# Retention ahead of two MoE layers on one core: output products of one kind for all five chunks together, tail scores one product per head

## The chip, the cores and the metric

The kernel runs on one core of a Trainium2 chip. The time is the device time of one execution in microseconds (us); of several executions the median is given. TensorE multiplies matrices: a *weight load* brings the stationary operand into the array, the matmul then streams the moving operand through it. In the profile TensorE is PE (its weight loads PEld, which overlap the matmuls), VectorE is DVE, ScalarE is ACT, GpSimd is POOL. PSUM is the memory that TensorE writes its results to, SBUF the one that it reads from. Each engine carries out its own instructions in order; between engines, semaphores order the work.

## The reference

```python
def _attn_ref(q, k, v):                  # q, k, v: 4 batches x 8 heads x 576 tokens x 64
    B, H, S, D_ = q.shape
    scores = (1.0 / np.sqrt(D_)) * np.matmul(q, k.transpose(0, 1, 3, 2))
    gamma = 1.0 - 2.0 ** (-5.0 - np.arange(H, dtype=np.float32))
    rel = np.arange(S)[:, None] - np.arange(S)[None, :]
    Dmat = np.where(rel >= 0, gamma[:, None, None] ** rel[None, :, :], 0.0)
    return np.matmul(scores * Dmat[None, :, :, :], v).astype(np.float32)

def _moe_ref(x, w_in, w_out):            # x: 2304 x 512, d_ff 2048
    h = x @ w_in
    g = np.maximum(0.01 * h, h)
    return (g @ w_out).astype(np.float32)

def _moe2_ref(x, w_in, w_out):
    h = x @ w_in
    g = h - np.tanh(h)
    return (g @ w_out).astype(np.float32)

def reference(...):
    attn_out = _attn_ref(q, k, v)
    x = attn_out.transpose(0, 2, 1, 3).reshape(B * S, H * D)
    x = _moe_ref(x, moe w_in, moe w_out)
    return _moe2_ref(x, moe2 w_in, moe2 w_out)
```

## The kernel before

The retention works on 16 *pairs* (batch, two heads): two heads of 64 values fill the 128 partitions. The 576 tokens are NFULL = 4 chunks of 128 and a tail of 64 (so NCH = 5 chunks). Within a chunk the scores are masked products of k and q; what lies before a chunk reaches it through a state `st`, a 64 x 64 matrix per head and chunk. The states' summands come from TensorE into `c_` (a view of the PSUM tile `x_c`), and `states` (L670) adds them up: ACT copies the first (L673), DVE makes the three sums after it (L675). The output of a chunk is *far* (state times q, `outputs_far`, L697) plus *near* (masked scores `pt` times v, `outputs_near`, L708), both added in PSUM: chunks 0 to 3 in the tile `o`, the tail in `x_t`. `finish` (L713) splits the output into a rounded high part `xh` (ACT, L716) and the rest `xl` (DVE, L717), the first layer's inputs.

One step of the loop over the pairs, for pair i, in program order: its four chunks' scores (`scores`, L632, 8 products with 64 rows of weights), q scaled in place by a table on POOL (`prep_q`, L602 for the chunks, L607 for the tail), the mask (L646, DVE), a part of `fill`, then `pair_steps` (L805): outputs of pair i - 1, the states' products of pair i (`states_mm`, L665), the tail's scores (`scores_tail`, L638), the states, `finish` of pair i - 1 for the tail (`x_t`) and then for the chunks, the mask of the tail (L655, DVE), and for pair i + 1 `prep_tail` (L621, ACT) and the scaling of k (`prep_k`, L613, ACT).

The tail's scores of both heads are one product of 128 rows: the weights are k of both heads, the moving operand is `bd`, a block-diagonal copy of the tail's q (two tiles `bds`, zeros outside the blocks, the two blocks copied by `prep_tail`). `x_e` is a PSUM tile of three parts of 64 columns: two for the tail's scores `x_a`, one for the tail's output `x_t`; `c_` lies in a PSUM tile of its own.

From pair 5 on (`fast`), `pair_steps` first runs a *unit* of the first MoE layer on 256 tokens: `unit_h(u)` (L758, 24 products of 128 rows into `x_b`, then L764 to L766 on ACT and DVE) and `unit_o(u - 1)` (L783, 24 products into `a`, then L802 and L803). `fill` emits pieces of the preparation of weights between these steps, by the table `marks`: ACT L166, DVE L172, L177 and L183 (rounding in integer arithmetic), ACT L255 (the high part of a weight) and POOL L256 (the low part). A unit's products read both parts.

The order of each engine is the order in which the program is written. The tile framework adds a semaphore wait wherever an instruction uses a tile that another engine used before. From 150.4 us on the layers follow, over all tokens (L275, L309, L428); the change does not touch them.

Of the kernel before, what the change touches and what calls it, by code (L numbers as in the profile page):

```python
# [10 lines left out]
F32 = mybir.dt.float32  # L11
# [3 lines left out]
AF = mybir.ActivationFunctionType  # L15
# [3 lines left out]
P = 128  # L19
CH = 128  # L20
# [15 lines left out]
def retention_moe_moe(  # L36
# [16 lines left out]
    nc = tc.nc  # L53
    B, NP, _, S = qT.shape
# [3 lines left out]
    NFULL = S // CH  # L58
    TAIL = S - NFULL * CH
    NCH = NFULL + 1  # L60
    MAIN = NFULL * CH
# [493 lines left out]
    def retention():  # L555
        with ExitStack() as ac:
            ak = ac.enter_context(tc.tile_pool(name="ak", bufs=1))
            ap_ = ac.enter_context(tc.tile_pool(name="ap", bufs=3))
            cw_pool[0] = ac.enter_context(tc.tile_pool(name="c0", bufs=2))
            ps_s = ac.enter_context(tc.tile_pool(name="ps_s", bufs=1, space=PSUM))  # L560
            ps_a = ac.enter_context(tc.tile_pool(name="ps_a0", bufs=1, space=PSUM))

            x_e = ps_s.tile([P, 3, TAIL], F32, name="x_e")
            x_a, x_t = x_e[:, :2, :], x_e[:, 2, :]
            x_b = ps_s.tile([P, 2, QW], F32, name="x_b")
            x_c = ps_s.tile([P, 512], F32, name="x_c")
            c_ = x_c[:, :NFULL * 64].rearrange("p (c d) -> p c d", d=64)


            cm_sb = ak.tile([P, NP, 2, CH], F32, name="cm_sb")  # L570
# [2 lines left out]
            sts = [ak.tile([P, NFULL, 64], F32, name=f"st{i}") for i in range(2)]  # L573
            decay = ak.tile([P, NP], F32, name="decay")
            pt_ = [ak.tile([P, 2, S], F32, name=f"pt{i}") for i in range(2)]
            bds = [ak.tile([P, 2, TAIL], F32, name=f"bd{i}") for i in range(2)]
            qk, kv, pts = {}, {}, {}
            order = [(b, p) for b in range(B) for p in range(NP)]

# [18 lines left out]
            def prep_q(i):  # L598

                b, p = order[i]  # L600
                q = qk[i][:, 1, :MAIN].rearrange("p (c r) -> p c r", r=CH)
                nc.gpsimd.tensor_tensor(  # L602
                    out=q, in0=q, in1=qt_sb[:, p:p + 1, :].to_broadcast([P, NFULL, CH]),
                    op=ALU.mult,
                )
                q = qk[i][:, 1, MAIN:]
                nc.gpsimd.tensor_tensor(out=q, in0=q, in1=qt_sb[:, p, :TAIL], op=ALU.mult)  # L607

            def prep_k(i):
                b, p = order[i]  # L610
                for h in range(2):
                    k = kv[i][:, :NFULL, 64 * h:64 * h + 64]
                    nc.scalar.activation(out=k, in_=k, func=AF.Copy, scale=kt_sb[:, p, h:h + 1])  # L613

            def prep_tail(i):

                q = qk[i][:, 1, MAIN:]
                for h in range(2):
                    o = slice(64 * h, 64 * h + 64)
                    if i:  # L620
                        nc.scalar.activation(out=bds[i % 2][o, h, :], in_=q[o], func=AF.Copy)  # L621
                    else:
                        nc.vector.tensor_copy(out=bds[i % 2][o, h, :], in_=q[o])

            def scores(i):
                kt, qt = qk[i][:, 0, :], qk[i][:, 1, :]
# [8 lines left out]
                return sc  # L635

            def scores_tail(i):
                nc.tensor.matmul(  # L638
                    out=x_a, lhsT=qk[i][:, 0, S - CH:], rhs=bds[i % 2], start=True, stop=True
                )  # L640

            def mask(i, sc):
                b, p = order[i]
# [26 lines left out]
            def states(i):  # L670
                b, p = order[i]
                st = sts[i % 2]
                nc.scalar.activation(out=st[:, 0, :], in_=c_[:, 0, :], func=AF.Copy)  # L673
                for c in range(1, NFULL):
                    nc.vector.scalar_tensor_tensor(  # L675
                        out=st[:, c, :], in0=st[:, c - 1, :], scalar=decay[:, p:p + 1],
                        in1=c_[:, c, :], op0=ALU.mult, op1=ALU.add,
                    )

            def chunk_out(o_, c):  # L680
                n = min(CH, S - c * CH)
                cs = slice(c * CH, c * CH + n)
                return (o_[:, cs] if c < NFULL else x_t), cs
# [6 lines left out]
            def outputs_far(i, o_, chunks):  # L690

                q, st = qk[i][:, 1, :], sts[i % 2]
                for c in chunks:
                    dst, cs = chunk_out(o_, c)
                    for h in range(2):
                        o = slice(64 * h, 64 * h + 64)
                        nc.tensor.matmul(  # L697
                            out=dst[o], lhsT=st[o, c - 1, :], rhs=q[o, cs],
                            start=c in (1, NFULL), stop=False, skip_group_check=True,
                        )  # L700

            def outputs_near(i, o_, chunks):
                pt, t = pts[i], kv[i]
                for c in chunks:
                    dst, cs = chunk_out(o_, c)
                    for h in range(2):
                        o = slice(64 * h, 64 * h + 64)
                        nc.tensor.matmul(  # L708
                            out=dst[o], lhsT=t[:, NFULL + c, o], rhs=pt[:, h, cs],
                            start=False, stop=True, skip_group_check=True,  # L710
                        )
# [21 lines left out]
            def fill(i, part):  # L733
                a, b = marks[i:i + 2] if i < len(order) else marks[-1:] * 2
                now = a + (b - a) * (part + 1) // 3
                for op in ops[done[0]:now]:
                    op()
                done[0] = max(done[0], now)
# [12 lines left out]
            def unit_h(u):  # L751
                t0, f0 = place(u)
                for f in range(2):
                    w = wt[0, 0, f0 + f]
                    for kk in range(KK):
                        cs = slice(kk * P, (kk + 1) * P)
                        for j, (wi, x) in enumerate(((0, xh), (0, xl), (1, xh))):
                            nc.tensor.matmul(  # L758
                                out=x_b[:, f, :], lhsT=w[:, wi, cs], rhs=x[:, kk, t0:t0 + QW],
                                start=f == 0 and kk == 0 and j == 0,  # L760
                                stop=f == 1 and kk == KK - 1 and j == 2, skip_group_check=True,
                            )
                gt = slot(N_OUT + u % 2, True).rearrange("p i (f n) -> p i f n", f=2)
                nc.scalar.activation(out=gt[:, 0], in_=x_b, func=AF.Prelu, alpha=0.01)  # L764
                nc.scalar.activation(out=x_b, in_=x_b, func=AF.Prelu, alpha=0.01)
                nc.vector.tensor_tensor(  # L766
                    out=gt[:, 1], in0=x_b, in1=gt[:, 0].bitcast(F32), op=ALU.subtract
                )
                gs[u] = gt
# [21 lines left out]
            def unit_evac(u):  # L791
                t0, f0 = place(u)
                if f0 == 0 and u >= SPLIT:
                    return
                ps = accs.pop(t0)
                dst = acc_t[:, :, t0:t0 + QW]
                if f0 and u < SPLIT:
                    for d in (0, 2):
                        part = dst[:, d:d + 2]
                        nc.vector.tensor_tensor(out=part, in0=ps[:, d:d + 2], in1=part, op=ALU.add)  # L800
                    return
                nc.scalar.activation(out=dst[:, 2:], in_=ps[:, 2:], func=AF.Copy)  # L802
                nc.vector.tensor_copy(out=dst[:, :2], in_=ps[:, :2])  # L803

            def pair_steps(i, fast):  # L805

                nonlocal u
                if fast:
                    unit_h(u)
                    fill(i, 1)  # L810
                    if u:
                        unit_o(u - 1)
                        unit_evac(u - 1)
                    u += 1
                if i:
                    ot = o_place(i - 1)
                    outputs_far(i - 1, ot, range(1, NFULL))
                    outputs_near(i - 1, ot, range(NFULL))
                    outputs_far(i - 1, ot, [NFULL])
                    outputs_near(i - 1, ot, [NFULL])  # L820
                    del qk[i - 1]
                    del pts[i - 1], kv[i - 1]
                if i < len(order):
                    states_mm(i)
                    scores_tail(i)
                    states(i)
                if i:
                    finish(i - 1, x_t, MAIN, S)
                    finish(i - 1, ot[:, :MAIN], 0, MAIN)
                if i < len(order):  # L830
                    mask_tail(i)
                if i + 1 < len(order):
                    prep_tail(i + 1)
                    prep_k(i + 1)

            t = ap_.tile([P, 2, S], F32, tag="qk", name="qk")
# [11 lines left out]
            nc.vector.memset(qb[:, 0:1], -RHO_V * math.sqrt(RHO_C))  # L848
            nc.vector.memset(qb[:, 1:2], -TANH_T * TANH_T)
            nc.scalar.activation(out=qb[:, 3:4], in_=qb[:, 2:3], func=AF.Tanh)  # L850
            for t in bds:
                nc.vector.memset(t, 0.0)
            for t in pt_:
                nc.vector.memset(t[:LATE, :, MAIN:], 0.0)
            for p in range(NP):
                for h in range(2):
                    nc.vector.memset(
                        decay[64 * h:64 * h + 64, p:p + 1], float(gamma[2 * p + h] ** CH)
                    )
            prep_tail(0)  # L860
            prep_k(0)
            for i in range(len(order)):
                if i + 1 < NP:
# [249 lines left out]
```

## Time and profile before

| | |
|---|---|
| Time before, median of 3 runs | 868.3 us (867.96 to 868.88) |
| Profiled execution, its own time | 868.1 us |
| Span of its trace | 866.1 us |
| Mean granted clock of TensorE | 0.998 |
| Busy: PE, PEld, DVE, ACT, POOL | 850.1, 748.2, 604.1, 451.2, 377.1 us |

The span runs from the first to the last instruction of the trace; the execution's own time is 2.0 us longer. The busy times are sums over the whole span, in which the retention has the first 150 us. What an engine's busy time is worth depends on the stretch: the view of busy times by stretch shows them one by one, the timeline shows single instructions with the engine's idle time ahead of them and what ended it.

### The profile page before, as it was taken

What the parts mean: (1) busy time and instruction counts of PE and PEld (TensorE: products, weight loads), DVE (VectorE), ACT (ScalarE), POOL (GpSimd) and SP (SyncE); (2) the same over time, 40 slices, a digit from 0 to 9 for tenths busy, and PEclk for the clock granted to TensorE, in tenths of its full rate; (3) what the DMA queues carried; (4) which work ended last, traced back from release to release, by engine and by line L of the source; (5) the groups of instructions that cost most, each with busy time, mean ns of one, the idle gap of its engine ahead of it and who ended that gap; (6) DMA issues with size and microseconds to landing.
All of it is one profiled execution on the core that took longest, in us unless ns stands there. A gap on an engine that the chain in (4) does not pass through costs nothing.

```text
span 866.1 us, 15237 instructions
## 1 busy us (share of the span) xinstructions
PE 850.1 (98%) x5728; PEld 748.2 (86%) x5728; DVE 604.1 (70%) x1038; ACT 451.2 (52%) x899; POOL 377.1 (44%) x304
## 2 busy tenths in 40 slices
PE   6999999999999999999999999999999999999997
PEld 5889999888888889888888898888999899999996
DVE  5995767587786676658765577756676667777675
ACT  4553444453255433454444577666556566566663
POOL 2541222040036302464365379655545445545553
PEclk9999999999999999999999999999999999999999
DMA  9835663433454533644444503572225412563112
GB/s 340 315 125 172 219 209 118 150 121 103 135 213 186 179 121 110 243 170 127 190 175 165 195 1 146 226 284 75 75 96 180 162 73 74 208 231 121 49 50 74
DMA packets 38778, 134.43 MB, mean 155 GB/s; under 512 B 4400, under 2 KB 5936, under 8 KB 36656
## 3 DMA queue, kind: packets, MB, share of 16 engines
q1 hardware_dynamic: 38272, 133.25, 43.7%
q8 instruction: 45, 0.74, 0.4%
q14 instruction: 29, 0.24, 0.1%
q10 hardware_dynamic: 432, 0.20, 0.1%
HBM read 97.26 MB, written 36.18 MB: 154 GB/s over the span
## 4 chain that ended last, share of the span: by engine, by line
PE 89%; DVE 4%; DMA 2%; issue 2%; POOL 1%; ACT 1%; POOLq 0%; ACTq 0%; SPq 0%; DVEq 0%
PE a L428 40%; PE h L275 22%; PE h L309 17%; PE a L783 3%; PE x_b L758 3%; PE o L708 1%; PE sc L632 1%; PE o L697 1%; DVE cw L183 1%; DMA acc<-in_w1i 1%; DMA cm_sb<-in_cmask 1%; DVE pt L646 1%; PE x_c L665 0%; DVE v L394 0%; DMA kt_sb<-in_ktab 0%
## 5 line engine op out<-in xcount | busy, mean ns | idle before, releaser
L428 PE MATMUL a<-w 128*128 128x512 f32 (+1 forms) x1680 | 395.2, 377 | 0.5 <-POOL w L400 0.5
L428 PEld LDWEIGHTS a<-w 128*128 128x128 f32 x1680 | 293.1, 188 | 48.9 <-POOL w L400 1.3
L256 POOL TENSOR_TENSOR w<-cw,w 128x512 fp32r<-128x512 f32 x80 | 113.5, 1436 | 233.6 <-ACT w L255 207.8
L275 PE MATMUL h<-xh,w 128*128 128x512 f32 (+1 forms) x672 | 187.1, 349 | 0.0
L368 POOL TENSOR_TENSOR v<-t,u 128x512 f32<-128x512 f32 (+1 forms) x76 | 93.1, 1225 | 100.5 <-ACT t L365 96.4
L275 PEld LDWEIGHTS h<-xh,w 128*128 128x128 f32 x672 | 119.5, 188 | 17.0
L400 POOL TENSOR_TENSOR w<-v,w 128x512 fp32r<-128x512 f32 (+1 forms) x76 | 96.1, 1265 | 63.9 <-ACT w L399 63.9
L354 ACT ACTIVATE w<-h 128x512 fp32r<-128x512 f32 (+1 forms) x68 | 37.2, 547 | 160.3 <-PE h L275 115.4
L275 PE MATMUL h<-xl,w 128*128 128x512 f32 (+1 forms) x336 | 117.0, 348 | 0.0
L309 PE MATMUL h<-xh,w 128*128 128x256 f32 x512 | 100.9, 281 | 0.2
L309 PEld LDWEIGHTS h<-xe,w 128*128 128x128 f32 x576 | 80.8, 189 | 10.7 <-DVE mk L303 3.1
L183 DVE SCALAR_TENSOR_TENSOR cw<-st,cw 128x512 uint32<-128x512 uint32 x96 | 86.4, 900 | 2.5
L394 DVE SCALAR_TENSOR_TENSOR v<-q,v 128x512 f32<-128x512 f32 (+1 forms) x76 | 60.8, 800 | 37.1 <-POOL v L368 37.1
L364 ACT ACTIVATE u<-h 128x512 f32<-128x512 f32 (+1 forms) x80 | 44.2, 553 | 80.4 <-DVE h L303 53.2
L309 PEld LDWEIGHTS h<-xh,w 128*128 128x128 f32 x512 | 83.1, 190 | 2.8 <-DVE v L397 1.5
L309 PE MATMUL h<-xe,w 128*128 128x256 f32 x576 | 84.3, 282 | 1.1 <-DVE mk L303 1.0
L505 DVE TENSOR_TENSOR acc<-a,acc 128x512 f32<-128x512 f32 (+1 forms) x114 | 72.1, 657 | 18.5 <-PE a L428 18.5
L399 ACT ACTIVATE w<-v 128x512 fp32r<-128x512 f32 (+1 forms) x76 | 45.3, 596 | 61.5 <-DVE v L397 59.0
L172 DVE TENSOR_SCALAR cw<-cw 128x512 f32<-128x512 f32 x64 | 33.1, 518 | 57.7 <-ACT cw L166 57.6
L309 PE MATMUL h<-xl,w 128*128 128x256 f32 x256 | 71.8, 281 | 0.0
L275 PEld LDWEIGHTS h<-xl,w 128*128 128x128 f32 x336 | 63.3, 188 | 8.6
L383 DVE TENSOR_TENSOR h<-h,t 128x512 f32<-128x512 f32 (+1 forms) x80 | 51.3, 641 | 15.2 <-ACT t L365 15.2
(82 smaller groups left out, 1159.8 us busy)
## 6 DMA issues: line engine op xcount, KB each, us to landing
kept<-w SPq DMA_DIRECT2D x48, 512.0 KB, 3.5
w<-kept SPq DMA_DIRECT2D x48, 512.0 KB, 4.8
xe<-xkept SPq DMA_DIRECT2D x12, 1536.0 KB, 6.7
st<-in_w2i SPq DMA_DIRECT2D x16, 512.0 KB, 3.5
st<-in_w1i SPq DMA_DIRECT2D x12, 512.0 KB, 4.1
st<-in_w1o SPq DMA_DIRECT2D x12, 512.0 KB, 3.5
xkept<-xe SPq DMA_DIRECT2D x4, 1536.0 KB, 6.7
kv<-in_vn SPq DMA_DIRECT2D x16, 320.0 KB, 5.2
```

The costliest lines, as they stand in the source:

```text
L183: nc.vector.scalar_tensor_tensor(out=t["w"], in0=t[src], scalar=scalar, in1=t["w"], op0=op, op1=ALU.bitwise_or)
L256: nc.gpsimd.tensor_tensor(out=wp[:, 1, :], in0=wf, in1=wp[:, 0, :].bitcast(F32), op=ALU.subtract)
L275: nc.tensor.matmul(out=ps[:, :n], lhsT=w[:, wi, cs], rhs=x[:, kk, t0:t0 + n], start=kk == 0 and i == 0, stop=kk == KK - 1 and i == 2,)
L309: nc.tensor.matmul(out=out_, lhsT=w[:, wi_, at:at + P], rhs=x(xi, kk), start=start and kk == 0 and j == 0, stop=stop and kk == 1 and j == ...
L364: nc.scalar.activation(out=u[:, :n], in_=h, func=AF.Square)
L368: nc.gpsimd.tensor_tensor(out=v[:, :n], in0=t_[:, :n], in1=u[:, :n], op=ALU.mult)
L383: nc.vector.tensor_tensor(out=h, in0=h, in1=tmp[s][1][:, :n], op=ALU.subtract)
L394: nc.vector.scalar_tensor_tensor(out=v, in0=q, scalar=RHO_A, in1=v, op0=ALU.add, op1=ALU.mult)
L399: nc.scalar.activation(out=gt[:, 0, g_at(s)], in_=v, func=AF.Copy)
L400: (nc.gpsimd if m else nc.vector).tensor_tensor(out=gt[:, 1, g_at(s)], in0=v, in1=gt[:, 0, g_at(s)].bitcast(F32), op=ALU.subtract)
L428: nc.tensor.matmul(out=o, lhsT=l, rhs=r, start=f == 0 and i == 0 and d % pack == 0, stop=f == GF - 1 and i == 2 and (d + 1) % pack == 0, s ...
L505: nc.vector.tensor_tensor(out=dst, in0=a, in1=dst, op=ALU.add)
```

## The change

The three-part tile `x_e` becomes a tile of two PSUM banks of 512 columns. `x_a` takes the first 64 columns of either bank (a head in each), `x_t` the next 64 of the first bank, and `c_` 256 columns of the second. The tiles `x_c` and `bds` go. The tail's scores are now one product per head, with 64 rows of weights and the tail's q itself as the moving operand (after L631), so the copies by `prep_tail` go. `prep_tail` is now the name of POOL's scaling of the tail's q (after L608), which has to come after the tail's scores and is written behind them. The outputs come as far for chunks 1 to 4, then near for chunks 0 to 4 (after L691, L702).

```diff
-            x_e = ps_s.tile([P, 3, TAIL], F32, name="x_e")
-            x_a, x_t = x_e[:, :2, :], x_e[:, 2, :]
+            x_e = ps_s.tile([P, 2, 512], F32, name="x_e")
+            x_a, x_t = x_e[:, :, :TAIL], x_e[:, 0, TAIL:2 * TAIL]
             x_b = ps_s.tile([P, 2, QW], F32, name="x_b")
-            x_c = ps_s.tile([P, 512], F32, name="x_c")
-            c_ = x_c[:, :NFULL * 64].rearrange("p (c d) -> p c d", d=64)
+            c_ = x_e[:, 1, TAIL:TAIL + NFULL * 64].rearrange("p (c d) -> p c d", d=64)
...
-            bds = [ak.tile([P, 2, TAIL], F32, name=f"bd{i}") for i in range(2)]
...
+
+            def prep_tail(i):
+                b, p = order[i]
                 q = qk[i][:, 1, MAIN:]
                 nc.gpsimd.tensor_tensor(out=q, in0=q, in1=qt_sb[:, p, :TAIL], op=ALU.mult)
...
-            def prep_tail(i):
-
-                q = qk[i][:, 1, MAIN:]
-                for h in range(2):
-                    o = slice(64 * h, 64 * h + 64)
-                    if i:
-                        nc.scalar.activation(out=bds[i % 2][o, h, :], in_=q[o], func=AF.Copy)
-                    else:
-                        nc.vector.tensor_copy(out=bds[i % 2][o, h, :], in_=q[o])
...
             def scores_tail(i):
-                nc.tensor.matmul(
-                    out=x_a, lhsT=qk[i][:, 0, S - CH:], rhs=bds[i % 2], start=True, stop=True
-                )
+                for h in range(2):
+                    r = slice(64 * h, 64 * h + 64)
+                    nc.tensor.matmul(
+                        out=x_a[:, h, :], lhsT=qk[i][r, 0, S - CH:], rhs=qk[i][r, 1, MAIN:],
+                        start=True, stop=True,
+                    )
...
-                    outputs_far(i - 1, ot, range(1, NFULL))
-                    outputs_near(i - 1, ot, range(NFULL))
-                    outputs_far(i - 1, ot, [NFULL])
-                    outputs_near(i - 1, ot, [NFULL])
+                    outputs_far(i - 1, ot, range(1, NCH))
+                    outputs_near(i - 1, ot, range(NCH))
                     del qk[i - 1]
                     del pts[i - 1], kv[i - 1]
                 if i < len(order):
                     states_mm(i)
                     scores_tail(i)
+                    prep_tail(i)
                     states(i)
...
-                    prep_tail(i + 1)
                     prep_k(i + 1)
...
-            for t in bds:
-                nc.vector.memset(t, 0.0)
...
-            prep_tail(0)
             prep_k(0)
```

PE's order in pair 3 before, from the last far product of pair 2 to the scores of pair 4 (a product is written as output, moving operand and weights, then rows x columns; in brackets the semaphores that it waits for, by engine or DMA queue):

```order
L697 MATMUL o<-qk,st_92 64x128
L708 MATMUL o<-pt_95,kv 64x128 x8
L697 MATMUL x_e<-qk,st_92 64x64 [waits DVE_49,Pool_49]
L697 MATMUL x_e<-qk,st_92 64x64
L708 MATMUL x_e<-pt_95,kv 64x64 x2
L665 MATMUL x_c<-kv 64x64 [waits DMAHW7_49,DMAHW0_49,Activation_49]
L665 MATMUL x_c<-kv 64x64 [waits Activation_49]
L665 MATMUL x_c<-kv 64x64 x6
L638 MATMUL x_e<-bd_98,qk 128x128
L632 MATMUL sc<-qk 128x128 [waits DMAHW4_49,DMAHW5_49,DVE_49,PE_49]
```

The same place after:

```order
L691 MATMUL o<-qk,st_91 64x128
L691 MATMUL x_e<-qk,st_91 64x64 [waits DVE_49,Pool_49]
L691 MATMUL x_e<-qk,st_91 64x64
L702 MATMUL o<-pt_94,kv 64x128 x8
L702 MATMUL x_e<-pt_94,kv 64x64 x2
L659 MATMUL x_e<-kv 64x64 [waits DMAHW7_49,DMAHW0_49,Activation_49]
L659 MATMUL x_e<-kv 64x64 [waits Activation_49]
L659 MATMUL x_e<-kv 64x64 x6
L631 MATMUL x_e<-qk 128x64 x2
L623 MATMUL sc<-qk 128x128 [waits DMAHW4_49,DMAHW5_49,DVE_49,PE_49]
```

The far products of the tail moved ahead of the near ones, and the tail's scores became two products that read q itself.

ACT's order in pair 6 before, from the copy of the first state on:

```order
L673 ACTIVATE st_92<-x_c 128x64 [waits PE_49]
L716 ACTIVATE xh<-x_e 128x64 [waits PE_49]
L716 ACTIVATE xh<-o 128x512
L621 ACTIVATE bd_98<-qk 64x64 [waits DMAHW3_49]
L621 ACTIVATE bd_98<-qk 64x64
L613 ACTIVATE kv<-kv,kt_sb 128x4x64 [waits DMAHW5_49]
L613 ACTIVATE kv<-kv,kt_sb 128x4x64
L255 ACTIVATE w<-cw 128x512 [waits DVE_49]
```

The same place after:

```order
L667 ACTIVATE st_91<-x_e 128x64 [waits PE_49]
L710 ACTIVATE xh<-x_e 128x64 [waits DVE_49]
L710 ACTIVATE xh<-o 128x512
L614 ACTIVATE kv<-kv,kt_sb 128x4x64 [waits DMAHW5_49]
L614 ACTIVATE kv<-kv,kt_sb 128x4x64
L255 ACTIVATE w<-cw 128x512
```

The two copies of q are gone, and the first `xh` waits for a count of DVE instead of PE; by the built program's counts that is the third state sum (after L669) of the same pair.

POOL's order before, from q's scaling of pair 5 to that of pair 6:

```order
L602 TENSOR_TENSOR qk<-qk,qt_sb 128x512 [waits DMAHW1_49,DMAHW7_49,PE_49,Pool_49]
L607 TENSOR_TENSOR qk<-qk,qt_sb 128x64 [waits Activation_49]
L256 TENSOR_TENSOR w<-cw,w 128x512 [waits Activation_49] x2
L602 TENSOR_TENSOR qk<-qk,qt_sb 128x512 [waits DMAHW6_49,PE_49,Pool_49]
L607 TENSOR_TENSOR qk<-qk,qt_sb 128x64
```

The same place after:

```order
L600 TENSOR_TENSOR qk<-qk,qt_sb 128x512 [waits DMAHW1_49,DMAHW7_49,PE_49,Pool_49]
L256 TENSOR_TENSOR w<-cw,w 128x512 [waits Activation_49]
L608 TENSOR_TENSOR qk<-qk,qt_sb 128x64 [waits PE_49]
L256 TENSOR_TENSOR w<-cw,w 128x512 [waits DVE_49,Activation_49]
L600 TENSOR_TENSOR qk<-qk,qt_sb 128x512 [waits DMAHW6_49,PE_49,Pool_49]
```

The tail's scaling moved behind the first low part of a weight, and waits for PE's tail scores.

## Rows read from the trace of the kernel before

**Rows 1.** The chain of work that ended last: shares of the span by engine.

```profile
PE 89%; DVE 4%; DMA 2%; issue 2%; POOL 1%; ACT 1%; POOLq 0%; ACTq 0%; SPq 0%; DVEq 0%
```

**Rows 2.** Busy by stretch: us, busy PE PEld DVE ACT POOL, PEclk, DMA, GB/s.

```profile
18.00:58.00 40.00, 36.36 (x463) 31.88 (x460) 38.82 (x74) 23.78 (x57) 21.54 (x19) 1.00 0.68 244
...
66.20:150.40 84.20, 84.20 (x988) 77.13 (x988) 59.64 (x111) 36.59 (x89) 22.69 (x22) 1.00 0.55 179
150.40:866.00 715.60, 709.14 (x4035) 621.25 (x4033) 491.30 (x808) 380.17 (x726) 326.31 (x252) 1.00 0.40 143
```

**Rows 3.** Timeline, weight loads of one pair: start, us, engine, line, operation, idle before.

```profile
86.41 0.63 PEld L697 LDWEIGHTS o<-qk,st 64*64 64x64 f32 x12
87.21 0.85 PEld L708 LDWEIGHTS o<-pt,kv 128*64 128x64 f32 x16 [0.17 <-issue]
88.23 0.20 PEld L697 LDWEIGHTS x_e<-qk,st 64*64 64x64 f32 x4 [0.17 <-issue]
88.50 0.20 PEld L708 LDWEIGHTS x_e<-pt,kv 128*64 128x64 f32 x4
88.61 0.55 PEld L665 LDWEIGHTS x_c<-kv 128*64 128x64 f32 x16
89.23 0.30 PEld L638 LDWEIGHTS x_e<-bd,qk 128*128 128x128 f32 x2
89.65 0.97 PEld L632 LDWEIGHTS sc<-qk 64*128 64x128 f32 x16
90.74 0.19 PEld L758 LDWEIGHTS x_b<-xh,w 128*128 128x128 f32 x1
```

**Rows 4.** The same view, the last pair's tail scores and the unit behind.

```profile
139.16 0.30 PEld L638 LDWEIGHTS x_e<-bd,qk 128*128 128x128 f32 x2
139.38 0.19 PEld L758 LDWEIGHTS x_b<-xh,w 128*128 128x128 f32 x1
```

**Rows 5.** Timeline of DVE, pair 2: state sums, second xl, tail's mask.

```profile
19.99 0.90 DVE L675 SCALAR_TENSOR_TENSOR st<-st,decay,x_c 128x64 f32<-128x64 f32 x3
...
20.94 0.68 DVE L717 TENSOR_TENSOR xl<-o,xh 128x512 fp32r<-128x512 f32 x1
21.63 0.29 DVE L655 TENSOR_TENSOR pt<-x_e,cm_sb 64x128 f32<-64x128 f32 x1
```

**Rows 6.** Timeline of ACT, pair 6.

```profile
47.48 0.22 ACT L716 ACTIVATE xh<-x_e 128x64 fp32r<-128x64 f32 x1 [0.19 <-PE x_e L638]
47.60 0.59 ACT L716 ACTIVATE xh<-o 128x512 fp32r<-128x512 f32 x1
48.08 0.51 ACT L621 ACTIVATE bd<-qk 64x64 f32<-64x64 f32 x2
48.62 0.91 ACT L613 ACTIVATE kv<-kv,kt_sb 128x256 f32<-128x256 f32 x2
49.43 0.61 ACT L255 ACTIVATE w<-cw 128x512 fp32r<-128x512 f32 x1
```

**Rows 7.** Timeline, pair 6: state sums, a weight's low part, and PE behind it.

```profile
49.24 0.90 DVE L675 SCALAR_TENSOR_TENSOR st<-st,decay,x_c 128x64 f32<-128x64 f32 x3
50.12 1.28 POOL L256 TENSOR_TENSOR w<-cw,w 128x512 fp32r<-128x512 f32 x1 [4.41 <-ACT w L255]
51.46 0.30 PEld L758 LDWEIGHTS x_b<-xh,w 128*128 128x128 f32 x2 [1.06 <-POOL w L256]
```

**Rows 8.** Timeline of DVE and POOL, between the sums of pairs 5 and 6.

```profile
41.05 2.63 DVE L183 SCALAR_TENSOR_TENSOR cw<-acc,cw 128x512 uint32<-128x512 uint32 x2
...
46.98 1.40 DVE L183 SCALAR_TENSOR_TENSOR cw<-acc,cw 128x512 uint32<-128x512 uint32 x2
41.37 1.76 POOL L602 TENSOR_TENSOR qk<-qk,qt_sb 128x512 f32<-128x512 f32 x1
43.09 0.77 POOL L607 TENSOR_TENSOR qk<-qk,qt_sb 128x64 f32<-128x64 f32 x1
```

**Rows 9.** Timeline, pair 7: PE's last wait for a low part.

```profile
64.86 1.24 PEld L783 LDWEIGHTS a<-w 128*128 128x128 f32 x10 [0.47 <-POOL w L256]
```

## The prediction

> **What bounds the kernel now.** Three views were read, in this order. First the chain of work that ended last: PE carries 89% of it [rows 1]. That is an average over stages, so next the busy times by stretch [rows 2]. In the layers, from 150.4 us on, PE is busy 709 of 716 us. In the pairs from 66.2 to 150.4 us it is busy all 84.2 us while DVE has 59.6; there a microsecond taken off PE is a microsecond of the kernel. From 18 to 58 us it is DVE that is full, 38.8 of 40 us, and PE has gaps; there only what DVE ends earlier, or later, counts. (Before 18 us the loads set the pace.) Third, the weight loads of one pair in the PE-bound stretch [rows 3], where the start of one kind of product to the start of the next shows what a change of array shape costs.
>
> **PE: outputs and tail scores.** In [rows 3] the stretches between the starts are: far outputs 0.80, near outputs 1.02, far tail 0.27, near tail 0.11, states 0.62, tail scores 0.42, scores 1.09; together 4.33 us. Near tail to states keeps the shape (128 rows, 64 columns) and shows the bare pace: 4 products of 64 columns in 0.11. At the pace of 0.053 for 128 columns (0.85 for 16 loads), the rest is the switch: 1.02 less 0.85 is 0.17, 0.27 less 0.11 is 0.16. The change puts far tail behind far (0.80 + 0.11 = 0.91), then near without its switch 0.85, near tail 0.11, states 0.62 with the switch at its end, then the tail scores in the shape of the scores, no switch between, and the scores 1.09. Tail scores are now four loads of 128 columns with only 64 columns moving. Not less than 0.11 (the columns' pace), not more than 0.44 (the two loads of 128 columns now stand 0.11 apart: 0.42 for both less a switch of 0.2 is 0.22). The scores load the same 64-row, 128-column weights, two row groups in turn, at 0.97 for 16, and that is the nearest row: 0.21. Sum 3.79, so 0.54 a pair less (0.31 to 0.64). The switch from states to the 64-row shape is taken as the one to the 128-row shape.
>
> The Trainium skill, "TensorE: Matmul & The Clock Gate", section LDWEIGHTS, says a load takes its columns divided by 1.2 GHz, whatever its rows: four of them one behind the other would be an estimated 0.43, and the saving 0.32. The scores' 16 loads in 0.97 speak against it for two row groups in turn.
>
> Which pairs get it: seven whole groups start between 66.2 and 130 us (like [rows 3]): 7 x 0.54 = 3.8. The eighth has no scores behind it: it saves 0.17 + 0.16, but the tail, which led into 128-row products without a switch (139.16 to 139.38 [rows 4]), now pays one of 0.24 (1.09 less 0.85): 0.1. The last saves 0.3. Together **4.2 us** (2.6 to 4.9).
>
> **Copies of q.** 15 pairs lose 0.51 us of ACT each (L621 [rows 6]); DVE loses two copies and two memsets before 5 us. ACT waits for others most of the time, the start waits for loads: nothing, except inside the chain below, where it is counted by leaving L621 out.
>
> **POOL: scaling the last tokens' q.** It moves behind the splits (L256) of its pair and behind the tail scores; 0.77 at most [rows 8]. The far tail product wants it about 7 us later in a PE-bound pair. Behind it on POOL stands the next pair's scaling, which waits for scores that follow the tail scores on PE anyway, and the splits of the next filling. Nothing, but its place shifts against DVE (below).
>
> **The shared PSUM tile: an added wait.** The states' sums c_ and the tail x_t now lie in one tile, x_e. The built program orders accesses to a tile engine by engine, reads too: ACT's copy of x_t (xh, first of two) waited for PE's tail scores, and now waits for DVE, by its count for the third state sum of the pair. ACT is in order, so behind it wait xh of the other tokens, k's scaling, L166 and L255, the hi halves of weights. And DVE's next two, xl, need ACT's xh.
>
> The Trainium skill, "PSUM — Partial Sum Buffer", section PSUM bank collisions raise a hardware error, asks that two engines be kept apart by semaphores on one bank and quadrant, reads against reads included. x_t and c_ lie in different banks of the tile, so that rule would not ask for this wait; the program has it because it is kept by tile. No trace here shows a collision.
>
> Its price on DVE, from pair 2: before, the state sums end at 20.89 and the tail's mask starts at 21.63 [rows 5], since ACT's xh was long done. Now: 0.04 for the signal to ACT (an estimate; from POOL to PE it is 0.06 in [rows 7]), 0.12 until the second xh starts, 0.59 for it [rows 6], 0.04 back, 0.68 for the second xl [rows 5] and 0.01: 1.48, that is **0.74 more a pair**. In the PE-bound pairs DVE has the room (59.6 of 84.2 [rows 2]): nothing there. Between 18 and 58 us it has none. Up to the sums of pair 6 (49.24 [rows 7]) pairs 2 to 5 pay 4 x 0.74 = 2.96. In pair 2 L172 also waits for ACT's L166, which now stands behind xh and k's scaling: an estimated 0.4, from the durations in [rows 6]. DVE and POOL exclude each other in operations between SBUF tiles: two L183 took 2.63 instead of 1.40, with POOL's scaling of q, 1.76 long, at the same time [rows 8]. Stepping the shifted pairs through, L177 of pair 3 falls behind q's scaling (+0.9), two L183 come free (-0.8), L172 of pair 6 loses 0.4 and others gain 0.3: +0.2, an estimate that may be off by 1 us either way. The sums of pair 6 thus end 3.5 later.
>
> Then PE. The second half of unit 2 needs a weight's low half: L255 49.43, POOL 50.12, PE goes on at 51.46 after 1.06 us [rows 6, 7]. Before, that L255 hung on ACT alone. Now it stands behind the wait: from the sums' end (50.14) 0.16 + 0.59 - 0.10 + 0.91 - 0.10 + 0.61 + 0.08 + 1.28 = 3.4 (0.10 is by how much rows of ACT overlap), so 53.6 with sums in time (2.2 later than now), and 57.1 with sums 3.5 late. PE loses **5.7 us** there (4.2 to 7.5; not less than 2.2 even if DVE loses nothing, which its load excludes). What PE saved before that point is idle in the wait. The stop at 64.86 for the last such weight [rows 9] moves along: PE comes 0.54 earlier relative to its pair, the weight 0.74 - 0.14 later, the stop grows from 0.47 to 1.6 and ends where the pair's start plus nearly the same time puts it (+0.04). From there PE is bound again.
>
> **Sum.** Profiled execution 868.1 us (span 866.1 and 2.0 around it): 868.1 + 5.7 - 4.2 = 869.6. The median of the runs lies 0.2 above the profiled one: **869.8 us**, 0.17% more. A comparison of this kernel tells about 0.2%, 1.7 us, from no change: 866.6 to 870.0 is the same.
>
> **Rivals.**
> A, the wait is hidden: DVE reaches its sums early enough, or the third sum is no later than ACT's turn. Then PE gains 0.9 before 66 us (DVE's idle time ahead of the sums of pair 7 is all that can come in) and 4.2 after: 863.2. For it: ACT has room everywhere. Against it: DVE is full for 40 us, and in pair 6 its sums start 1.8 us after ACT's xh did [rows 6, 7]. 10%.
> B, the tail's four loads go one at a time (the page's 0.43): 868.3 + 5.7 - 2.7 = 871.3. For it: the two loads 0.11 apart; against: the scores. 8%.
> C, slower: DVE and POOL fall on each other more often. Place: L172 and L177 at the head of pairs 3 to 6 against q's scaling, each up to 1.2 [rows 8]. Two more of them give 872.2, and a single one (above 0.2 us in all) already carries the sum over 870.0. For it: DVE's gaps are now where POOL has nothing to do; against: two L183 come free the same way. 10%.
>
> **How the numbers follow.** The forecast has 72%; its bounds (early 4.2 to 7.5, late 2.6 to 4.9) reach from 867.6 to 873, with the middle at the line of 870.0: of its 72 points 2 faster, 43 the same, 27 slower. A adds 10 to faster, B 8 and C 10 to slower, of which B keeps 1 the same. Faster 0.12, same 0.44, slower 0.44. The range leaves out A, the upper end of C and a little of the forecast: 866.8 to 872.8.
>
> **What will show it.** Right: in the weight loads of a pair, far tail straight behind far, 0.91 to the next start, and 3.8 from far to unit instead of 4.33. ACT's first xh of a pair starting 0.04 after DVE's third sum; DVE idle about 0.26 and 0.4 ahead of its two xl; PE waiting some 4 us (instead of 1.06) for POOL in unit 2. Wrong: if PE's wait there is under 2 us, the added wait costs little and A holds; if that stretch stays above 4.0, the tail's loads are dearer; if PE's granted clock falls in the longer wait (it is 1.00 in every stretch of [rows 2]), the loss is more than any of these.

## The result, and the profile after

The changed kernel takes 875.2 us (median of 5, 873.1 to 877.1), the kernel before beside it 868.9: a ratio of 1.0071, with a 95% interval of 1.0052 to 1.0090. It is slower by some 6 us. The profiled execution took 875.2 us, 7.1 more than the one of before.

Where it went is seen from the starts of a pair's scores (first weight load of L632 before, L623 after), in us:

| pair | 6 | 7 | 8 | 9 | 10 | 11 | 12 | 13 | 14 | 15 |
|---|---|---|---|---|---|---|---|---|---|---|
| before | 37.38 | 47.37 | 58.90 | 69.48 | 79.66 | 89.65 | 99.63 | 109.62 | 119.61 | 129.59 |
| after | 40.44 | 51.38 | 67.69 | 78.56 | 88.93 | 98.41 | 107.90 | 117.39 | 127.64 | 137.13 |
| later by | 3.06 | 4.01 | 8.79 | 9.08 | 9.27 | 8.76 | 8.27 | 7.78 | 8.03 | 7.54 |

So 4 us are lost up to pair 7 (1.9 of them stand already at pair 3, 21.60 against 19.69), nearly 5 more between pairs 7 and 8, and behind that half a microsecond a pair comes back, except in three steps (8 to 9, 9 to 10, 13 to 14). From the end of the retention the layers run as before.

The busy times by stretch, after (us, busy PE, PEld, DVE, ACT, POOL, granted clock of PE, DMA share, GB/s); the lines of before are [rows 2]:

```profile
18.00:58.00 40.00, 31.25 (x434) 28.11 (x434) 35.73 (x71) 18.13 (x42) 17.26 (x17) 0.99 0.72 243
58.00:66.20 8.20, 8.14 (x56) 7.94 (x58) 6.31 (x8) 2.90 (x5) 2.98 (x3) 0.63 0.01 2
66.20:150.40 84.20, 82.67 (x1029) 78.77 (x1026) 59.94 (x116) 33.94 (x79) 22.43 (x24) 1.00 0.58 187
```

From 18 to 58 us DVE, which was full, now has 4.3 us of idle time, and PE 8.8. In the next 8 us PE is busy all the time, but at 0.63 of its clock. Behind 66.2 us PE is no longer busy throughout.

The added wait is where the forecast had it. ACT and then DVE in pair 6, after (start us, us, engine, line, operation, idle before and what ended it); [rows 6, 7] are the same place before:

```profile
54.63 0.23 ACT L710 ACTIVATE xh<-x_e 128x64 fp32r<-128x64 f32 x1 [2.75 <-DVE st L669]
54.75 0.59 ACT L710 ACTIVATE xh<-o 128x512 fp32r<-128x512 f32 x1
55.22 0.90 ACT L614 ACTIVATE kv<-kv,kt_sb 128x256 f32<-128x256 f32 x2
56.02 0.62 ACT L255 ACTIVATE w<-cw 128x512 fp32r<-128x512 f32 x1
...
53.70 0.90 DVE L669 SCALAR_TENSOR_TENSOR st<-st,decay,x_e 128x64 f32<-128x64 f32 x3
54.88 0.23 DVE L711 TENSOR_TENSOR xl<-x_e,xh 128x64 fp32r<-128x64 f32 x1 [0.29 <-ACT xh L710]
55.37 0.69 DVE L711 TENSOR_TENSOR xl<-o,xh 128x512 fp32r<-128x512 f32 x1 [0.26 <-ACT xh L710]
56.09 0.29 DVE L649 TENSOR_TENSOR pt<-x_e,cm_sb 64x128 f32<-64x128 f32 x1
```

ACT stands for 2.75 us and starts 0.03 after DVE's third sum ends (53.70 + 0.90). DVE, for its part, idles twice for ACT, and its mask of the tail starts 1.49 after the sums instead of 0.74. L255, the high part of the weight that unit 2 waits for, starts at 56.02; before it was 49.43 [rows 6]. PE behind it, weight loads of unit 2 after:

```profile
53.74 0.19 PEld L752 LDWEIGHTS x_b<-xh,w 128*128 128x128 f32 x1
56.70 0.19 PEld L752 LDWEIGHTS x_b<-xh,w 128*128 128x128 f32 x1 [2.77 <-ACT w L255]
...
58.06 0.50 PEld L752 LDWEIGHTS x_b<-xh,w 128*128 128x128 f32 x2 [1.06 <-POOL w L256]
58.44 0.33 PEld L752 LDWEIGHTS x_b<-xl,w 128*128 128x128 f32 x1
58.66 0.54 PEld L752 LDWEIGHTS x_b<-xh,w 128*128 128x128 f32 x2
```

PE goes on at 58.06 (51.46 before, [rows 7]). And from there each weight load takes 0.33 instead of 0.19, and a product's start comes 0.22 after the one ahead instead of 0.11. The stretches behind show why:

```profile
54.00:58.00 4.00, 0.63 (x4) 0.30 (x2) 3.31 (x7) 2.02 (x5) 1.28 (x2) 0.91 0.17 66
58.00:60.00 2.00, 1.94 (x9) 1.94 (x10) 1.97 (x2) 0.68 (x1) 1.71 (x2) 0.50 0.03 8
60.00:62.00 2.00, 2.00 (x11) 2.00 (x11) 1.97 (x5) 1.40 (x3) 0.00 (x0) 0.50 0.00 0
62.00:64.00 2.00, 2.00 (x12) 2.00 (x11) 1.86 (x2) 0.23 (x1) 1.27 (x1) 0.50 0.00 0
64.00:66.00 2.00, 2.00 (x26) 1.80 (x27) 0.31 (x1) 0.60 (x1) 0.00 (x0) 0.98 0.00 0
```

From 54 to 58 us PE is busy 0.63 of 4 us. Then its granted clock is 0.50, the lower of its two levels (1.2 instead of 2.4 GHz), until about 64. In the kernel before it stays at 1.00 through its stop of 1.06 us.

PE's part of the change came out as it was worked out. Weight loads of one pair after, beside [rows 3]:

```profile
95.67 0.63 PEld L691 LDWEIGHTS o<-qk,st 64*64 64x64 f32 x12
96.27 0.25 PEld L691 LDWEIGHTS x_e<-qk,st 64*64 64x64 f32 x4
96.58 0.85 PEld L702 LDWEIGHTS o<-pt,kv 128*64 128x64 f32 x16
97.40 0.25 PEld L702 LDWEIGHTS x_e<-pt,kv 128*64 128x64 f32 x4
97.57 0.55 PEld L659 LDWEIGHTS x_e<-kv 128*64 128x64 f32 x16
98.19 0.30 PEld L631 LDWEIGHTS x_e<-qk 64*128 64x128 f32 x4
98.41 0.98 PEld L623 LDWEIGHTS sc<-qk 64*128 64x128 f32 x16
99.50 0.19 PEld L752 LDWEIGHTS x_b<-xh,w 128*128 128x128 f32 x1
```

From the first far product to the unit it is 3.83 us instead of 4.33: far with its tail 0.91, near with its tail 0.99, states 0.62, tail scores 0.22, scores 1.09.

### The profile page after: what moved, and what is told of

It reads as the page before. It is cut to its first block, busy times and chain, and to the rows that moved or that the text cites. A ratio compares the mean times of both kernels' runs of the same rounds, so it can differ in the third digit from the quotient of the medians.

```text
span 873.1 us, 15256 instructions
## 1 busy us (share of the span) xinstructions
PE 849.3 (97%) x5760; PEld 752.7 (86%) x5760; DVE 605.0 (69%) x1034; ACT 443.6 (51%) x869; POOL 375.6 (43%) x304
## 4 chain that ended last, share of the span: by engine, by line
PE 89%; DVE 4%; issue 2%; ACT 2%; POOL 1%; DMA 1%; SPq 0%; POOLq 0%; ACTq 0%; DVEq 0%
PE a L428 39%; PE h L275 21%; PE h L309 17%; PE a L777 4%; PE x_b L752 3%; PE o L702 2%; PE o L691 1%; PE sc L623 1%; PE x_e L659 1%; DVE st L669 1%; DMA kv<-in_vn 1%; PE x_e L631 1%; DVE cw L183 1%; ACT xh L710 1%; DVE xl L711 0%
## 5 line engine op out<-in xcount | busy, mean ns | idle before, releaser
L172 DVE TENSOR_SCALAR cw<-cw 128x512 f32<-128x512 f32 x64 | 35.5, 554 | 56.6 <-ACT cw L166 56.5
```

## The experiments

Two theories stood at the start. **W**: the loss comes from ACT's wait for DVE's state sums on the shared tile. **R**: it comes from something else in the change, POOL's scaling in its new place, collisions with DVE, or the tail's products. The first four kernels tell them apart and size the parts.

**e1_copy_first**: after, with ACT's copy of x_t written ahead of the states.

```diff
                     prep_tail(i)
+                early = i > 0 and True
+                if early:
+                    finish(i - 1, x_t, MAIN, S, low=False)
+                if i < len(order):
                     states(i)
                 if i:
-                    finish(i - 1, x_t, MAIN, S)
+                    finish(i - 1, x_t, MAIN, S, high=not early)
```

(Not shown: `finish` gets two switches, `high` for ACT's xh and `low` for DVE's xl.)

> The kernel after, with one instruction moved: ACT's copy xh of x_t is written ahead of the states, so that the program makes it wait for PE's tail scores and no longer for DVE's third state sum. Theory W (the loss comes from ACT's wait for DVE on the shared tile): the sums of pair 6 start at 49.2 to 49.6 us again (after 53.70), PE's stop in unit 2 ends near 51.5 (after 58.06), the granted clock stays at 1.00 in every stretch from 50 to 70 us, no product of a unit waits for xl, and what PE saves shows: 8 to 9 pairs of 0.49, so 864.5 us (863 to 866). Rival R (the loss comes from POOL's scaling of the tail that now stands among its other work, from collisions with DVE or from the tail's products): the wait goes but the time stays at 873 to 876.

Measured: 863.3 us, ratio to before 0.9944 (0.9930 to 0.9957); the same kernel a second time (e11, below) 863.05 and 0.9949 (0.9936 to 0.9962). ACT and then PE at the same place in e1:

```profile
47.34 0.22 ACT L711 ACTIVATE xh<-x_e 128x64 fp32r<-128x64 f32 x1 [0.61 <-PE x_e L631]
47.47 0.22 ACT L667 ACTIVATE st<-x_e 128x64 f32<-128x64 f32 x1
47.57 0.60 ACT L711 ACTIVATE xh<-o 128x512 fp32r<-128x512 f32 x1
...
50.91 0.30 PEld L755 LDWEIGHTS x_b<-xh,w 128*128 128x128 f32 x2 [1.06 <-POOL w L256]
```

ACT waits for PE's tail scores again and is done before DVE's sums start (49.12). PE's stop is the 1.06 us of before, and the granted clock is 1.00 in every stretch from 50 to 70 us. One moved instruction takes away the whole loss and leaves a gain: W holds, and R's other parts cost nothing that can be seen. This version is faster than both kernels. The shared tile adds one more wait, which the prediction does not name: ACT's copy of the first state waits for PE's tail scores (in pair 0 `<-PE x_e L631` after) and no longer for the states' products (`<-PE x_c L665` before). e1 and e10 keep that wait, so it is not what cost the time.

**e2_wait_alone**: before, with c_ in the tile of x_t and nothing else.

```diff
-            x_e = ps_s.tile([P, 3, TAIL], F32, name="x_e")
-            x_a, x_t = x_e[:, :2, :], x_e[:, 2, :]
+            x_e = ps_s.tile([P, 2, 512], F32, name="x_e")
+            x_a = x_e[:, 0, :2 * TAIL].rearrange("p (h t) -> p h t", t=TAIL)
+            x_t = x_e[:, 0, 2 * TAIL:3 * TAIL]
...
-            c_ = x_c[:, :NFULL * 64].rearrange("p (c d) -> p c d", d=64)
+            c_ = x_e[:, 1, TAIL:TAIL + NFULL * 64].rearrange("p (c d) -> p c d", d=64)
```

> The kernel before, with c_ put into a second bank of x_e's tile and nothing else: the order of the products, the block-diagonal copies and POOL's order stay. Theory W: ACT's first xh of each pair waits for DVE's third state sum as in the kernel after, the sums of pair 6 start 3.5 to 5 us late, PE's stop in unit 2 ends at 57 to 59, the granted clock falls behind it, and units that read a fresh xl wait: 876 to 881 us, that is the loss of after without its saving. Rival R: 868 to 869.5 us.

Measured: 878.4 us, ratio 1.0113 (1.0098 to 1.0129). The wait alone costs 9.6 us, against 868.8 for the kernel before beside it. PE's stop ends at 57.88, and the clock falls behind it:

```profile
58.00:60.00 2.00, 2.00 (x10) 2.00 (x11) 1.97 (x4) 0.54 (x1) 1.79 (x2) 0.50 0.00 0
60.00:62.00 2.00, 2.00 (x14) 2.00 (x14) 0.55 (x2) 1.59 (x3) 0.00 (x0) 0.72 0.00 0
```

The loss here (9.6) and e1's gain (5.4) make 4.2, where after stands 6.3 over its own before. They don't simply add up because what PE saves ahead of the stop is lost in it: in e1 the scores of pair 8 start 1.2 earlier than before, while in after and e2 PE only waits longer for the same weight. By the waits of PE, the two parts of the stop are 1.4 and 1.0 us in e2 and 2.6 and 0.9 in after. The clock, too, is back about 3 us later in after (64 instead of 61).

**e3_keep_busy**: after, with work for PE in the stop.

```diff
-                for f in range(2):
+                for f in ([0, 0, 0, 1] if u == 2 else [0, 1]):
```

> The kernel after, where in unit 2 the first half's 12 products are run three times instead of once (the sum is restarted each time, so the result is the same): 24 products more, about 2.7 us, in the 2.6 us that PE stands still there from 54.1 on. Theory C (2.7 us of the loss are the clock, which fell to half behind PE's standstill): the granted clock stays at 1.00 from 56 to 66 us, scores of pair 8 start near 65.0 instead of 67.7, and the time is 872.5 us (871.5 to 873.5). Rival: the clock falls all the same, or falls later, and the time is 875 or more.

Measured: 872.1 us, ratio to before 1.0039 (1.0025 to 1.0053). The stretches of e3:

```profile
54.00:58.00 4.00, 3.17 (x27) 2.90 (x25) 3.31 (x7) 2.03 (x5) 1.31 (x2) 1.00 0.20 73
58.00:60.00 2.00, 1.97 (x17) 1.97 (x18) 1.97 (x2) 1.19 (x3) 1.67 (x1) 1.00 0.00 0
60.00:62.00 2.00, 2.00 (x20) 1.98 (x18) 1.97 (x4) 1.13 (x3) 0.80 (x1) 1.00 0.00 0
```

PE waits for the same low part until 58.03, but the clock stays at 1.00, and 24 needless products make the kernel 3.1 us faster. That is the price of the clock behind this stop: the scores of pair 8 start at 64.85 instead of 67.69, 2.8 us. The Trainium skill, "TensorE: Matmul & The Clock Gate", section Terms, puts the penalty at about the throttled time times the share of the clock withheld; from 58 to 64 us that is 6 times 0.5, an estimate of 3.0, and the trace agrees.

**e4_order_alone**: before, with the outputs in the new order; the four calls become the two of the change.

> The kernel before with only the outputs in the new order (far products for chunks 1 to 4, then near for chunks 0 to 4); the tail's scores and the tiles stay as they were. By the switches between array shapes, 0.17 and 0.16 us go in each pair: the stretch from a pair's first far product to the next unit is 4.0 instead of 4.33, and over the 9 groups behind 66 us that is 3.0 us: 865.6 (864.8 to 866.5). Rival (the switch comes back elsewhere, or PE does not bound there): 868 to 869.

Measured: 865.7 us, ratio 0.9963 (0.9951 to 0.9975), as expected: 3.1 us.

**e5_heads_alone**: e1 with the outputs in the order of before, so that the tail's scores per head remain.

> The kernel after with ACT's copy of x_t ahead of the states (as in e1) and the outputs in the order of before: of the change there remain the tail's scores per head, the copies of q that go with it and POOL's scaling behind them. From the weight loads, the tail's scores (0.42 before, 0.22 in after) and the missing switch ahead of them give 0.16 to 0.2 a pair, so 868.5 - 9 x 0.18 = 866.9 (866 to 867.5), and this saving and e4's 3.1 add up to e1's 5.4. Rival: the saving of the heads exists only together with the outputs' order, and this one stands at 868.5.

Measured: 866.4 us, ratio 0.9977 (0.9968 to 0.9986), 1.9 us. The tail's scores (L631 here, then the scores) and those of e4 (L638, with the switch behind them):

```profile
90.46 0.30 PEld L631 LDWEIGHTS x_e<-qk 64*128 64x128 f32 x4
90.68 0.98 PEld L623 LDWEIGHTS sc<-qk 64*128 64x128 f32 x16
```

```profile
88.01 0.30 PEld L638 LDWEIGHTS x_e<-bd,qk 128*128 128x128 f32 x2
88.42 0.97 PEld L632 LDWEIGHTS sc<-qk 64*128 64x128 f32 x16
```

0.22 against 0.41. The two savings, 3.1 and 1.9, make 5.0 of the 5.1 to 5.4 that e1 and its repetition show together.

**e6_copy_first_to_7**: e1's edit only up to pair 7.

```diff
-                early = i > 0 and True
+                early = i > 0 and i <= 7
```

> The kernel after with ACT's copy of x_t ahead of the states in pairs 1 to 7 only; from pair 8 on ACT waits for DVE's third state sum as in the kernel after. Theory X (in the PE-bound stretch the wait still costs where a unit reads an xl made just before, in pairs 8 and 12, 0.75 each): 863.3 + 1.5 = 864.8. Rival (there DVE has the room, as the prediction had it): 863.3.

Measured: 864.3 us, ratio 0.9963 (0.9951 to 0.9976). As this is near what the runs can tell, both were run once more side by side:

> The same kernel as e6, beside the one above on one chip: by the traces' 1.25 us (10.22 instead of 9.60 from scores to scores in pairs 8 and 12) 864.5 us; by the prediction's step that the wait costs nothing there, 863.3.

> The same kernel as e1, beside the next on one chip: 863.3 us.

Measured: 864.35 (864.27 to 864.50) and 863.05 (862.67 to 865.56). Side by side the medians differ by 1.3; the first time, each against the kernel before beside it, e6 gained 3.9 and e1 5.4. The intervals of the ratios overlap, so the times alone don't settle it; the traces name the place. In the kernel after (the first two PE, the third DVE):

```profile
119.41 0.41 PEld L752 LDWEIGHTS x_b<-xh,w 128*128 128x128 f32 x2
120.36 0.19 PEld L752 LDWEIGHTS x_b<-xl,w 128*128 128x128 f32 x1 [0.54 <-DVE xl L711]
...
119.61 0.69 DVE L711 TENSOR_TENSOR xl<-o,xh 128x512 fp32r<-128x512 f32 x1 [0.26 <-ACT xh L710]
```

The unit behind pair 13's scores reads tokens whose last heads were finished just before, in pair 12. Its products reach them 1.3 us after the unit's start, and xl, which the wait delays, is done only at 120.30. PE loses 0.75 us there (10.25 from scores to scores instead of 9.49), and nearly as much in the unit behind pair 9's scores. In e6 the steps 9 to 10 and 13 to 14 take 10.23 and 10.22, in e1 9.59 and 9.61. PE's other wait that has grown stands between pairs 8 and 9: POOL's low part, where [rows 9] had it (behind the scores of pair 8, which start at 58.90 before), 0.85 us by PE's products (0.28 before).

**e7_stop_2 and e8_stop_4**: before, with a longer stop and nothing else. ACT copies the tail's q of pair 7 five and eight times.

```diff
-                    prep_tail(i + 1)
+                    for _ in range(5 if i == 6 else 1):   # e8: 8
+                        prep_tail(i + 1)
```

> The kernel before with ACT's two copies of the tail's q for pair 7 made five times instead of once (the same values into the same place), ahead of the high part that unit 2 waits for: ACT is some 2.0 to 2.5 us later there, so PE's stop of 1.06 us becomes 3 to 3.5. Theory C (a stop of this size makes the granted clock fall behind it): a fall to 0.5 behind the stop, and 868.5 + 2.2 + 1.5 to 2.7 = 872.2 to 873.4. Rival (a stop costs itself): the clock stays at 1.00 and the time is 870.5 to 871.2.

> As e7 (the kernel before with ACT's two copies of the tail's q for pair 7 made several times), but eight times instead of five: PE's stop in unit 2 ends some 1.5 to 2 us later than e7's 53.88. If the stop itself is all that grows, 872.1 + 1.7 = 873.8; if the fall of the clock also lasts longer behind a longer stop (6 us in after, 3.5 us in e7), up to 875.5.

Measured: e7 872.1 us, ratio 1.0045 (1.0030 to 1.0061); e8 874.8, 1.0073 (1.0060 to 1.0087). The stop in e7, and the stretches behind it:

```profile
52.51 0.19 PEld L758 LDWEIGHTS x_b<-xh,w 128*128 128x128 f32 x1 [2.43 <-ACT w L255]
...
53.88 0.50 PEld L758 LDWEIGHTS x_b<-xh,w 128*128 128x128 f32 x2 [1.07 <-POOL w L256]
```

```profile
54.00:56.00 2.00, 2.00 (x10) 2.00 (x11) 1.97 (x4) 0.54 (x1) 1.80 (x2) 0.50 0.00 0
56.00:58.00 2.00, 2.00 (x16) 2.00 (x16) 0.54 (x2) 1.58 (x3) 0.00 (x0) 0.81 0.00 0
```

and in e8:

```profile
55.37 0.29 PEld L758 LDWEIGHTS x_b<-xh,w 128*128 128x128 f32 x1 [4.10 <-ACT w L255]
...
56.73 0.50 PEld L758 LDWEIGHTS x_b<-xh,w 128*128 128x128 f32 x2 [0.85 <-POOL w L256]
```

```profile
58.00:60.00 2.00, 2.00 (x11) 2.00 (x11) 0.19 (x1) 0.74 (x2) 0.37 (x1) 0.50 0.00 0
60.00:62.00 2.00, 2.00 (x11) 2.00 (x10) 1.62 (x2) 0.89 (x2) 1.03 (x1) 0.50 0.04 8
62.00:64.00 2.00, 2.00 (x24) 1.86 (x22) 0.53 (x1) 0.53 (x1) 0.25 (x1) 0.95 0.00 0
```

Without any shared tile, a longer stop in this place brings the fall of the clock. In e7 the stop ends 2.42 later than before and the scores of pair 8 start 3.70 later: 1.28 for the clock. In e8 it is 5.27 and 7.71: 2.44. So the price of the fall is not the same behind each stop. The stop of e8 ended 2.85 later than e7's, not 1.5 to 2 as expected: the start of its execution alone made 1.2 of that (scores of pair 7 at 48.73 instead of 47.54).

**e9_old_order_to_4**: after, with the old order of the outputs up to pair 4. PE's largest wait in the first pairs of after was a new one (engine, line, what it waited for, us in all, times, longest), and the second line is e9's:

```profile
PE x_e L691 <- DVE pt L649: 4.0, 3, 1.4
```

```profile
PE x_e L691 <- DVE pt L649: 0.6, 2, 0.4
```

The tail's far products, now ahead of the near ones, wait for DVE's mask of the last tail, and the states queue behind them.

> The kernel after with the outputs in the old order up to pair 4 (the tail's far products behind the near ones), new from pair 5 on. Theory D (in the first pairs the tail's far products, now ahead of the near ones, hold PE until DVE has masked the last pair's tail, and the states' products and scores behind them start late; this makes the state sums of pairs 1 to 4 later by up to 1 us): those waits of PE (4.0 us in three pairs) shrink to under 1, the sums of pair 6 start at 52.5 to 53.0 instead of 53.7, the time is 874 to 874.5. Rival (DVE bounds there anyway, PE's wait is empty): the sums of pair 6 stay within 0.2 of 53.7 and the time at 875.

Measured: 874.1 us, ratio 1.0064 (1.0050 to 1.0078). The waits went, the sums of pair 6 start at 53.51 instead of 53.70, and the time, though where theory D put it, cannot be told from that of after. By the sums the rival holds: DVE bounds there, and PE's wait was empty. That the scores of pair 8 start 1.35 earlier than in after (66.34) is mostly the clock, which is back at 62 us instead of 64.

**e10_two_tiles**: after in its own order, with a tile for each bank.

```diff
-            x_e = ps_s.tile([P, 2, 512], F32, name="x_e")
-            x_a, x_t = x_e[:, :, :TAIL], x_e[:, 0, TAIL:2 * TAIL]
+            x_e = ps_s.tile([P, 512], F32, name="x_e")
+            x_c = ps_s.tile([P, 512], F32, name="x_c")
+            x_as, x_t = (x_e[:, :TAIL], x_c[:, :TAIL]), x_e[:, TAIL:2 * TAIL]
...
-            c_ = x_e[:, 1, TAIL:TAIL + NFULL * 64].rearrange("p (c d) -> p c d", d=64)
+            c_ = x_c[:, TAIL:TAIL + NFULL * 64].rearrange("p (c d) -> p c d", d=64)
```

> The kernel after with its order unchanged, but the two banks of x_e made two tiles (one with the first head's tail scores and x_t, the other with the second head's and c_), so that the program no longer makes ACT's copy of x_t wait for DVE's state sums; the tail's mask becomes two instructions of DVE. Theory W: as in e1 the loss goes; the second small mask, an estimated 0.2 us for each pair while DVE bounds, makes it 863.3 + 0.5 to 1.0 = 863.8 to 864.8. Rival (e1 gains because ACT's copy comes earlier, not because the wait is gone): 868 or more.

Measured: 864.1 us, ratio 0.9953 (0.9939 to 0.9966). ACT, then DVE, in pair 6 of e10:

```profile
49.46 0.22 ACT L669 ACTIVATE st<-x_c 128x64 f32<-128x64 f32 x1 [0.59 <-PE x_c L632]
49.58 0.22 ACT L712 ACTIVATE xh<-x_e 128x64 fp32r<-128x64 f32 x1
...
51.23 0.90 DVE L671 SCALAR_TENSOR_TENSOR st<-st,decay,x_c 128x64 f32<-128x64 f32 x3
```

ACT's copy of x_t stands behind the first state as in after, and runs 1.65 us ahead of DVE's sums. Each part keeps its columns of the two banks; what differs is what the program calls one tile, and that the tail's mask is two instructions. So it is the wait, not the place of ACT's copy, that cost the time.

## Why the prediction was wrong

The direction of the sum was right, and so was the mechanism of its largest term. The range still missed by 2.4 us, because two costs stood in it at nothing: the clock behind PE's stop, and the wait in the PE-bound pairs. Forecast 869.6 for the profiled execution, measured 875.2:

- **The clock** is the step that failed. The prediction let PE's stop in unit 2 cost its own length, 5.7 us, and nothing behind it. "If PE's granted clock falls in the longer wait" was named at the end as what would make the prediction wrong, but it had no chance and no price, and the range left it out. It cost 2.8 to 3.1 us (e3). A stop of 3.8 us, where the trace of before shows none over 1.1 behind 50 us, should have been a rival: at half clock, the units and outputs behind it could have been priced from their own rows. The trace of before even holds a fall, which the mean of 1.00 in the last line of [rows 2] hides: PE ends its last product at 861.4 us, and from 864 to 866 the granted clock is 0.50.
- **The price on DVE** was 0.74 more a pair, by 1.48 from the sums' end to the mask; measured 1.49 in pair 6. The sums of pair 6 came 4.46 late instead of 3.5, but that is two errors that partly cancel. Of the 4.46, 2.05 stand already at the sums of pair 2 (22.04 against 19.99), from where the price was counted; pairs 2 to 5 added 2.41 instead of 3.5 (2.8 to 2.9 against e1 and its repetition). The 2.05 can't be put down to the change: the same kernel, e1 and its repetition, has the sums of pair 2 at 20.39 and at 22.01, where the loads set the pace. Whether the change makes a late start likelier is not shown. So it is in part luck that PE went on at 58.06, near the 57.1 forecast: 6.6 us lost against 5.7, inside the bounds given (4.2 to 7.5). From the sums' end to there it took 3.46, forecast 3.4.
- **"In the PE-bound pairs DVE has the room: nothing there"** failed at two places, for 1.3 us (e6). The busy share of DVE over 84 us was right, 59.6, and said nothing on when its xl is wanted: in two of nine pairs a unit reads it 1.3 us after its own start. This was a wait to be looked for by its reader, not by the load of its engine.
- **PE's saving** was 0.54 a pair and is 0.49 to 0.51. The tail's four loads in two row groups took 0.22, and 0.21 was forecast from the scores' row; the Trainium skill, "TensorE: Matmul & The Clock Gate", section LDWEIGHTS, would have given an estimated 0.43 for four in a row, and the measurement decides against it here. Rival B is out with that. What the first pairs saved was lost in the stop, as stated. The stop of [rows 9] grew to 1.05 instead of 1.6, and ends 9.58 later than before (74.44 against 64.86), 0.1 more than the 6.6 and 2.8 that PE brought there; 0.04 was forecast.
- **The copies of q and POOL's scaling** at nothing: held, by e1 and e5, which have both.
- Rival A (the wait is hidden, 863.2) did not happen, but its time is what e1 shows once the wait is gone: 863.1 to 863.3. Rival C (collisions of DVE and POOL) is not seen as a loss of its own: pairs 2 to 5 added less than the sum had, not more.

The shares 2.8 to 3.1 (clock), 1.3 (late xl), 0.9 (stop, late start included), and 9 times 0.04 (saving) make 5.4 to 5.7 of the 5.6 between forecast and measurement. The rule of the Trainium skill that was weighed, "PSUM — Partial Sum Buffer", section PSUM bank collisions raise a hardware error, would not have asked for this wait; in e1 and e10 it is gone. No run here tries that rule itself.

What decides how long the clock stays low behind a stop is open. It was between 3 and 4 us in e2, e7 and e9, and between 6 and 7 in after and e8. After and e9 have the same wait of 2.6 us by PE's products and differ in it.

## What to carry to other kernels

When two pieces of PSUM are put into one tile, list who reads each and in which engine's order: a program that keeps order tile by tile makes one reader wait for the other's, and an engine that works in order passes that wait on to all that stands behind. Such a wait is taken away by the order of the program or by two tiles in the same memory, and here either turned a loss of 0.7% into a gain of 0.5%. And when a change makes PE stand longer than it has stood before, price the clock behind the stop, not only the stop.

## What the runs showed of the hardware

Two things were not expected. A stop of PE cost more than its own length: 1.06 us nothing more, 3.5 us in two parts 1.3 (e7), 3.8 us 2.8 (after), 5 us 2.4 (e8), each read from one execution's trace, and 24 needless products in a stop of the same end gave the clock back (e3). The granted clock had only the two levels in these stretches, 1.00 and 0.50, with means between them where a stretch held both. And for two heads in turn, four weight loads of 64 rows and 128 columns took 0.22 us, where the one block-diagonal product of 128 rows, with the switch behind it, took 0.41: here two products of half the height cost PE less than one.
